# A state-space convolution beside a gated linear unit: the input's spectrum stored once, and its exchanged copy made by ScalarE

## The chip, the core and the metric

The kernel runs on one core of a Trainium2 chip. Its time is the device time of one execution in microseconds (us). The engines have these names in the profile: PE is TensorE (matmul), PEld its weight loads, DVE VectorE, ACT ScalarE, POOL GpSimd; SP issues all the transfers. The on-chip memory SBUF and the accumulators PSUM have 128 partitions.

## What is computed

With L = 2048 positions, D = 448 channels, N = 256 states and F = 1792 hidden units, all fp32:

```python
def _A_ref(u, log_A_real, A_imag, C_real, C_imag, log_dt, D_skip):   # L = 2048
    dt = jnp.exp(log_dt)
    A = -jnp.exp(log_A_real) + 1j * A_imag
    C = (C_real + 1j * C_imag) * dt[:, None]
    P = jnp.exp((A * dt[:, None])[:, :, None] * pos[None, None, :])
    K = 2.0 * jnp.einsum("dn,dnl->dl", C, P).real
    y = jnp.fft.irfft(jnp.fft.rfft(u_t, 2 * L) * jnp.fft.rfft(K, 2 * L), 2 * L)[:, :, :L]
    return y.transpose(0, 2, 1) + u * D_skip
def _B_ref(x, w_gate, w_up, w_down):
    h = _sigmoid(x @ w_gate) * (x @ w_up)
    return h @ w_down
g = _sigmoid((x * gate_w).sum(-1, keepdims=True))
return g * _A_ref(x, ...) + (1 - g) * _B_ref(x, ...)
```

Path A makes a long filter K for each channel and convolves u with it by Fourier transforms; path B is a gated linear unit (GLU) on the same input; a gate mixes the two.

## The kernel before

**Path A.** The channels are worked in two halves of 224. A transform of 4096 points is split into a stage of 64-point transforms (`stage1`, L812), an exchange of 32x32 blocks between partitions (`transpose`), and a stage of 32-point transforms (`spectrum_four`, L845). A `Chain` object carries one half through these stages in one tile `fx` of 128 x 32 x 224. A row of 64 partitions of a spectrum has 32 real rows and then 32 imaginary rows; the matrix `m_sb` holds the 32-point transform forwards, backwards, and a third form of it.

First the chains of u run, one for each half, in the pool `fu` (`fx_fu`). Their spectra go to DRAM, to `us0` and `us1`. Meanwhile `kgen` makes K in 28 chunks (tiles `tb`, `es`, `cs`, `nn`, `ke`) and stores it to `kd0` and `kd1`. Then the chains of K run: chain 0 in `fx_fu` with tiles `uax`, chain 1 in `fx_fk` with tiles `ua`. In `product` each takes eight blocks b: it loads the block of u's spectrum into a tile of [128, 2, 2, 448] (two buffers for each chain), makes the spectrum of K in PSUM by matmuls (L845), multiplies on DVE (L879), transforms back by matmuls (L889, `product_four`), and ACT evacuates into `fx` (L762). `back` does the last stage (L924) after another `transpose`, which chain 0 does through DRAM (`shf`) and chain 1 on DVE (L826).

A complex product needs each of K's rows times u's real part and times u's imaginary part. The kernel before stores the real rows of u's spectrum twice, one copy under the other, as c = 0, and the imaginary rows twice as c = 1. So `ua[:, 0]` is (real, real) and `ua[:, 1]` is (imaginary, imaginary), each loaded by a transfer of 448 KB, and the inverse transform of c = 1 uses the third matrix, `turned`.

**Path B.** `glu_up` (L1423 to L1428, tiles `gu`) and `glu_down` (L1443 to L1447, tiles `dn`) do the GLU in fp32 from rounded high and low parts: ACT rounds a part (`wh`, `vh`, `hh`, L1388 and L1414), DVE takes the remainder (`wl`, `vl`, `hl`), ACT does tanh (`sg`, L1407), and DVE sums up in `ob` (L1462). TensorE has GLU matmuls between the pieces of path A over the whole run, to the end.

**The order of the work.** The table `PLACE` gives each operation of each engine its place in that engine's queue, by engine, tile and priority; `Plan.order` merges these queues with a model of the costs, and `emit` writes the instructions out. An engine runs its queue strictly in this order. The numbers were found by a search outside of this file. All transfers are issued by SP, in its own order. The helper that records a transfer is line L712, and that of an evacuation L762.

Of the kernel before, what the change touches and what calls it, by code (L numbers as in the profile page):

```python
# [13 lines left out]
AF = mybir.ActivationFunctionType  # L14
# [4 lines left out]
L, D, N, F = 2048, 448, 256, 1792  # L19
# [9 lines left out]
    ('Act', 'aci', 10): (14, 40,),  # L29
    ('Act', 'aci', 19): (65, 94,),  # L30
    ('Act', 'acr', 10): (15, 39, 49,),
    ('Act', 'acr', 19): (63, 91, 101,),
# [26 lines left out]
    ('Act', 'dots', 1): (28,),  # L59
    ('Act', 'dots', 2): (45,),  # L60
    ('Act', 'dots', 16): (67, 83,),
# [18 lines left out]
    ('Act', 'idn', 10): (12,),  # L80
    ('Act', 'junk', 10): (29, 60,),
    ('Act', 'junk', 19): (77, 81, 132,),
# [12 lines left out]
    ('Act', 'pos_sb', 10): (36, 52,),  # L95
# [22 lines left out]
    ('DVE', 'aci', 10): (45,),  # L118
    ('DVE', 'aci', 19): (122,),
    ('DVE', 'acr', 10): (89,),  # L120
    ('DVE', 'acr', 19): (152,),
# [1467 lines left out]
```

## Time and profile before

| | |
|---|---|
| runs, median (lowest to highest of 3) | 688.12 us (686.7 to 689.95) |
| profiled execution | 684.96 us |
| its span, first to last instruction | 683.0 us |
| mean granted TensorE clock | 0.999 |
| moved by transfers | 122.79 MB, mean 180 GB/s |

The profile is of one execution. Its page gives the busy time of each engine, the chain of work that ended last, and groups of instructions; further views give waits, a timeline, and busy time by stage. In the timeline a row has a start, a duration (of all its instructions together, xcount), the engine, the line and the tiles, and in brackets the idle time ahead of it with what ended that. In a row of groups the numbers behind the bar are busy us and mean ns of one instruction. Rows of transfers have the size and the median time from issue to landing. Durations of one engine overlap: how fast a queue moves is seen from the distance of starts.

The stages by time: parameters and gate until about 115 us, `kgen` until 505 us with the chains of u in it, the products of both chains from 530 to 626 us, the transforms back from 647 us.

### The profile page before, as it was taken

To read this page: it belongs to the slowest core of one execution; us is meant where nothing else is said; L and a number is where in the kernel's file an instruction comes from. 1 tells how busy PE (TensorE), PEld (TensorE's weight loads), DVE (VectorE), ACT (ScalarE), POOL (GpSimd) and SP (SyncE) were. 2 spreads that over 40 slices of the span, in tenths; PEclk is the share of its full clock that TensorE was granted. 3 is DMA by queue.
4 is the path that set the end of the run, shared out by engine and by line. 5 is a ranking of instruction groups with operands and counts; after the bars stand their busy time and mean duration, and the time that the engine had idled before them with its cause. 6 is when DMAs were issued, how large, how long until landed. Compare 5 with 4: busy or idle time off the path is not lost.

```text
span 683.0 us, 16235 instructions
## 1 busy us (share of the span) xinstructions
PE 669.7 (98%) x6568; PEld 480.6 (70%) x6568; DVE 603.7 (88%) x699; ACT 509.7 (75%) x928; POOL 269.2 (39%) x280
## 2 busy tenths in 40 slices
PE   8899999999999999999989999999999999999997
PEld 7677667877886687776646666778878766546864
DVE  7998999999899999999998999999974379667976
ACT  6588799898999999999999999999842442333110
POOL 0506486555466656675856567643000000000000
PEclk9999999999999999999999999999999999999999
DMA  8869432683793999737977884343968981888855
GB/s 265 222 146 245 111 101 57 174 217 139 208 173 85 204 203 225 237 111 178 176 211 179 200 212 113 124 155 111 204 133 217 280 292 66 300 276 217 153 141 129
DMA packets 96898, 122.79 MB, mean 180 GB/s; under 512 B 31032, under 2 KB 80504, under 8 KB 95800
## 3 DMA queue, kind: packets, MB, share of 16 engines
q1 hardware_dynamic: 96824, 121.76, 69.7%
q8 instruction: 52, 0.85, 0.5%
q14 instruction: 22, 0.18, 0.1%
HBM read 78.16 MB, written 43.58 MB: 178 GB/s over the span
## 4 chain that ended last, share of the span: by engine, by line
PE 82%; DVE 10%; ACT 3%; DMA 2%; issue 2%; SPq 1%; DVEq 0%
PE gu_gps L1423 10%; PE gu_gps L1424 9%; PE gu_gps L1425 9%; PE kp_egp L1290 7%; PE dn_gps L1443 6%; PE dn_gps L1445 5%; PE tp_egp L1232 4%; PE tp_egp L1241 4%; PE dn_gps L1446 4%; PE dn_gps L1447 4%; PE fps_fups L812 3%; PE gu_gps L1427 3%; PE fps_fups L845 3%; PE gu_gps L1428 3%; PE fps_fups L889 2%; PE fps_fkps L889 2%
## 5 line engine op out<-in xcount | busy, mean ns | idle before, releaser
L1423 PE MATMUL gu_gps<-xs_glu,wh_glu 128*128 128x512 f32 x336 | 144.6, 430 | 1.6 <-DVE hl_glu L1409 0.8
L1278 DVE TENSOR_TENSOR cs_eg<-cs_eg,es_eg 128x2048 f32<-128x2048 f32 x56 | 131.5, 2349 | 1.4
L1424 PE MATMUL gu_gps<-xs_glu,wh_glu 128*128 128x512 f32 x336 | 132.0, 393 | 0.1
L1425 PE MATMUL gu_gps<-xs_glu,wl_glu 128*128 128x512 f32 x336 | 131.7, 392 | 0.0
L1222 POOL TENSOR_TENSOR tb_eg<-tb_eg 128x96 f32<-128x96 f32 (+2 forms) x84 | 118.8, 1416 | 6.1
L1261 DVE TENSOR_TENSOR es_eg<-tb_eg 128x1024 f32<-128x1024 f32 x112 | 110.4, 1013 | 2.1 <-POOL tb_eg L1222 0.5
L1423 PEld LDWEIGHTS gu_gps<-xs_glu,wh_glu 128*128 128x128 f32 x336 | 63.2, 188 | 30.8 <-issue 15.8
L1275 DVE TENSOR_TENSOR cs_eg<-cs_eg,es_eg 128x1024 f32<-128x1024 f32 x56 | 70.8, 1264 | 8.2 <-ACT cs_eg L1254 5.8
L1238 ACT ACTIVATE nn_eg<-cs_eg 128x512 fp32r<-128x512 f32 x112 | 74.9, 669 | 3.8 <-PE tp_egp L1241 2.6
L1407 ACT ACTIVATE sg_glu<-gu_gps 128x512 f32<-128x512 f32 x56 | 34.5, 615 | 55.2 <-PE gu_gps L1428 54.9
L1424 PEld LDWEIGHTS gu_gps<-xs_glu,wh_glu 128*128 128x128 f32 x336 | 63.3, 188 | 16.0 <-issue 5.0
L1425 PEld LDWEIGHTS gu_gps<-xs_glu,wl_glu 128*128 128x128 f32 x336 | 63.1, 188 | 14.4
L1243 ACT ACTIVATE cs_eg<-tp_egp 128x512 f32<-128x512 f32 x112 | 70.0, 636 | 3.1 <-PE tp_egp L1241 2.7
L1236 ACT ACTIVATE cs_eg<-tp_egp 128x512 f32<-128x512 f32 x112 | 69.9, 633 | 2.7 <-PE tp_egp L1232 1.0
L1244 ACT ACTIVATE cs_eg<-tp_egp 128x512 f32<-128x512 f32 x112 | 69.0, 627 | 1.1 <-PE tp_egp L1241 1.1
L1254 ACT ACTIVATE cs_eg<-cs_eg,half_pi 128x1024 f32<-128x1024 f32 x56 | 66.7, 1191 | 0.2
L1225 POOL TENSOR_TENSOR tb_eg<-tb_eg,bs_eg 128x32 f32<-128x32 f32 x84 | 62.6, 745 | 6.4
L1462 DVE SCALAR_TENSOR_TENSOR ob_glu<-dn_gps,og,ob_glu 128x448 f32<-128x448 f32 x70 | 47.4, 677 | 16.0 <-PE dn_gps L1447 15.1
L1290 PEld LDWEIGHTS kp_egp<-cs_eg 128*32 128x32 f32 x3584 | 51.3, 110 | 10.7 <-issue 7.6
L1212 POOL MEMSET tb_eg<- 128x96 f32 x28 | 8.0, 287 | 127.9 <-DVE es_eg L1261 124.8
L1290 PE MATMUL kp_egp<-cs_eg 128*32 128x64 f32 x3584 | 55.8, 220 | 0.0
L1241 PE MATMUL tp_egp<-nn_eg,idn 128*128 128x512 f32 x112 | 51.4, 459 | 1.2 <-ACT nn_eg L1238 1.2
(168 smaller groups left out, 1326.0 us busy)
## 6 DMA issues: line engine op xcount, KB each, us to landing
shf<-fx_fu SPq DMA_DIRECT2D x16, 896.0 KB, 5.4
fx_fu<-shf SPq DMA_DIRECT2D x16, 896.0 KB, 10.4
us<-fx_fu SPq DMA_DIRECT2D x16, 896.0 KB, 9.7
xr_glu<-in_w_dram SPq DMA_DIRECT2D x46, 256.0 KB, 6.1
uax_fk<-us SPq DMA_DIRECT2D x16, 448.0 KB, 4.3
ua_fk<-us SPq DMA_DIRECT2D x16, 448.0 KB, 6.0
xr_glu<-in_w_dram SPq DMA_DIRECT2D x17, 224.0 KB, 4.1
gt_pre<-in_u_dram SPq DMA_DIRECT2D x8, 448.0 KB, 6.9
```

Of the source, the lines that this page charges most:

```text
L1222: pool(96 * m, lambda n=n, m=m: G.tensor_mul(g3(n + 1, m), g3(1, m), g3(n, 1).to_broadcast([128, 32, 3, m])))
L1236: op("Act", c_act(512, True), lambda: S.activation(cs[:, 1, ds, 32:96], block(tp), AF.Copy, bias=MAGIC), [tp], [(cs, ("s", i))], prio)
L1238: op("Act", c_act(512), lambda: S.activation(block(nn), cs[:, 1, ds, 32:96], AF.Copy, scale=-1.0, bias=MAGIC), [(cs, ("s", i))], [nn], prio)
L1241: op("PE", c_mm(532), lambda: T.matmul(tp.real, idn.real, nn.real, start=False, stop=True, skip_group_check=True), [nn, idn], [tp], prio)
L1243: op("Act", c_act(512, True), lambda: S.activation(cs[:, 0, ds, 32:96], block(tp), AF.Abs), [tp], [(cs, ("c", i))], prio)
L1261: V.tensor_mul(o.rearrange("p d (i k) -> p d i k", k=ny), x.unsqueeze(3).to_broadcast([128, 16, nx, ny]), y.unsqueeze(2).to_broadcast([128 ...
L1275: op("DVE", c_dve(1024), lambda: V.tensor_mul(cs[:, :, :, 0:32], cs[:, ::-1, :, 63:31:-1], es[:, :, 0:32].unsqueeze(1).to_broadcast([128, ...
L1278: op("DVE", c_dve(2048), lambda: V.tensor_mul(cs[:, :, :, 32:96], cs[:, :, :, 32:96], es[:, :, 32:96].unsqueeze(1).to_broadcast([128, 2, 1 ...
L1290: T.matmul(kp[32 * j:32 * j + 32, q], cs[:, z, 4 * j + q, 64:96], cs[:, z, 4 * j + q, 0:64], start=cs is parts[0] and z == 0 and q == 0, s ...
L1423: T.matmul(p.real, wh[:, k, cs], x[:, k], start=(k == 0), stop=False)
L1424: T.matmul(p.real, wh[:, k, cs], x[:, 4 + k], start=False, stop=False)
L1425: T.matmul(p.real, wl[:, k, cs], x[:, k], start=False, stop=False)
```

## The change

The spectrum of u is stored as it is, with real rows over imaginary rows, once: four stores for each half in place of eight. `product` loads it once for each block, as `ua[:, 0]` = (real, imaginary). The second copy `ua[:, 1]` = (imaginary, real) is made on chip by `turn_parts`: for each of two halves z of the tile's columns, ACT copies four groups of 32 partitions to the neighbouring group. The tables follow: the product of c = 0 is now (real x real, imaginary x imaginary), and the signs are moved into the matrices. Lines behind the new function are 6 higher than before.

```diff
     inv[re, re], inv[im, re], inv[re, im], inv[im, im] = cw, -sw, sw, cw
-    turned[re], turned[im] = inv[im], -inv[re]
+    turned[re], turned[im] = inv[im], inv[im]
+    inv[im] = -inv[re]
...
-    us = [dt_([128, 2, 8, 2 * D], f"us{h}") for h in halves]
+    us = [dt_([128, 8, 2 * D], f"us{h}") for h in halves]
...
-            for q in range(2):
-                for g in range(2):
-                    for c in range(2):
-                        dma(lambda q=q, g=g, c=c: us[64 * g:64 * g + 64, c, 4 * q:4 * q + 4].rearrange(
-                                "(z k) b f -> k z (b f)", z=2),
-                            lambda q=q, g=g, c=c: x[64 * g + 32 * c:64 * g + 32 * c + 32, 16 * q:16 * q + 16].rearrange(
-                                "k l d -> k (l d)").unsqueeze(1).to_broadcast([32, 2, 8 * D]),
-                            64 * 16 * HD * 4, self.keys(8 * q, 8 * q + 8), [(us, (q, g, c))], prio, 215.0, 1400.0)
+            for q in range(4):
+                dma(lambda q=q: us[:, 2 * q:2 * q + 2].rearrange("p b f -> p (b f)"),
+                    lambda q=q: x[:, 8 * q:8 * q + 8].rearrange("p l d -> p (l d)"), 128 * 8 * HD * 4,
+                    self.keys(4 * q, 4 * q + 4), [(us, q)], prio)
...
                 ua = self.tile("ua", (128, 2, 2, D))
+                dma(lambda ua=ua: ua[:, 0].rearrange("p z f -> p (z f)"), lambda b=b: us[:, b], 128 * 2 * D * 4,
+                    [(us, b // 2)], [(ua, (0, 0)), (ua, (0, 1))], self.prio)
                 for c in range(2):
-                    dma(lambda ua=ua, c=c: ua[:, c].rearrange("p z f -> p (z f)"), lambda b=b, c=c: us[:, c, b],
-                        128 * 2 * D * 4, [(us, (b // 4, g, c)) for g in range(2)], [(ua, (c, 0)), (ua, (c, 1))], self.prio)
+                    self.turn_parts(ua, c)
                 self.product_four(ua, b)
...
+        def turn_parts(self, ua, z):
+            def f():
+                for a in range(0, 128, 32):
+                    to = a ^ 32
+                    S.activation(ua[to:to + 32, 1, z], ua[a:a + 32, 0, z], AF.Copy)
+            op("Act", 4 * c_act(D), f, [(ua, (0, z))], [(ua, (1, z))], self.prio)
```

The table `PLACE` has new numbers throughout, of which one line shows the kind:

```diff
-    ('SP', 'us0', 30): (135, 136, 132, 131, 140, 141, 139, 137,),
+    ('SP', 'us0', 30): (130, 135, 136, 138,),
```

ScalarE's queue in the middle of the products. Before, it holds the evacuations of the inverse transforms of both chains (L762), with a GLU instruction between (L1407 tanh, L1388 rounding):

```order
L762 ACTIVATE fx_fk_6562<-fps_fkps_7070 128x448
L762 ACTIVATE fx_fk_6562<-fps_fkps_7069 128x448
L1407 ACTIVATE sg_glu_7132<-gu_gps_7005 128x512
L762 ACTIVATE fx_fk_6562<-fps_fkps_7122 128x448
L762 ACTIVATE fx_fu_5091<-fps_fups_7134 128x448
L762 ACTIVATE fx_fk_6562<-fps_fkps_7121 128x448
L762 ACTIVATE fx_fu_5091<-fps_fups_7135 128x448
```

Now the copies of both chains (L879 of the new file) stand between the evacuations (L763 of the new file); this is the place of chain 1's blocks 5, 6 and 7 (`ua_fk_7272`, `7333`, `7392`):

```order
L879 ACTIVATE uax_fk_7285<-uax_fk_7285 32x448 x4
L763 ACTIVATE fx_fu_4932<-fps_fups_7349 128x448
L763 ACTIVATE fx_fu_4932<-fps_fups_7350 128x448
L763 ACTIVATE fx_fk_6536<-fps_fkps_7375 128x448
L879 ACTIVATE uax_fk_7285<-uax_fk_7285 32x448 x4
L879 ACTIVATE ua_fk_7333<-ua_fk_7333 32x448 x8
L879 ACTIVATE ua_fk_7392<-ua_fk_7392 32x448 x4
L763 ACTIVATE fx_fu_4932<-fps_fups_7436 128x448
L763 ACTIVATE fx_fk_6536<-fps_fkps_7376 128x448
```

The second evacuation of one block (`fps_fkps_7376`) now stands sixteen copies and an evacuation behind the first (`fps_fkps_7375`).

SP's queue in the same stretch. Before, two transfers for each block, among the stores of chain 0's `transpose` (`shf`):

```order
L712 DMA uax_fk_7080<-us_58 128x896
L712 DMA ua_fk_7090<-us_59 128x896
L712 DMA shf<-fx_fu_5091 128x1792
L712 DMA ua_fk_7090<-us_59 128x896
L712 DMA uax_fk_7080<-us_58 128x896
L712 DMA ua_fk_7145<-us_59 128x896
```

Now one for each, with loads of GLU weights (`xr`) between them:

```order
L713 DMA uax_fk_7019<-us_58 128x896
L713 DMA ua_fk_7066<-us_59 128x896
L713 DMA xr_glu_7069<-in_w_dram 128x512
L713 DMA uax_fk_7100<-us_58 128x896
L713 DMA xr_glu_7118<-in_w_dram 128x448
L713 DMA ua_fk_7126<-us_59 128x896
```

Each block's second transfer is gone; its place in the chain of a block is taken by the copies on ScalarE. In all SP's queue goes from 328 rows to 304, ScalarE's gets 128 instructions more, and TensorE's has the same 2,303 matmul rows in a new order.

More of the change, by code (lines that the diff above doesn't have):

```diff
@@ L28 @@
 PLACE = {
[L29 to L32, printed above, removed]
[26 rows of a table removed]
-    ('Act', 'dots', 1): (28,),
-    ('Act', 'dots', 2): (45,),
-    ('Act', 'dots', 16): (67, 83,),
[18 rows of a table removed]
-    ('Act', 'idn', 10): (12,),
-    ('Act', 'junk', 10): (29, 60,),
-    ('Act', 'junk', 19): (77, 81, 132,),
[12 rows of a table removed]
-    ('Act', 'pos_sb', 10): (36, 52,),
[13 rows of a table removed]
+    ('Act', 'aci', 10): (15, 41,),
+    ('Act', 'aci', 19): (67, 101,),
+    ('Act', 'acr', 10): (16, 38, 52,),
@@ L109 @@
+    ('Act', 'acr', 19): (64, 97, 110,),
[26 rows of a table added]
+    ('Act', 'dots', 1): (28,),
+    ('Act', 'dots', 2): (46,),
+    ('Act', 'dots', 16): (66, 80,),
[18 rows of a table added]
+    ('Act', 'idn', 10): (14,),
+    ('Act', 'junk', 10): (32, 60,),
+    ('Act', 'junk', 19): (76, 81, 136,),
[12 rows of a table added]
+    ('Act', 'pos_sb', 10): (35, 40,),
[11 rows of a table added]
+    ('Act', 'uax', 40): (829, 828, 842, 832, 852, 865, 871, 869, 883, 880, 898, 890, 906, 900, 916, 912,),
[3 rows of a table added]
     ('Act', 'wh', 0): (1, 4,),
     ('Act', 'wh', 1): (6, 7,),
[4 rows of a table removed]
[4 rows of a table added]
     ('Act', 'xs', 0): (0, 2, 3, 5,),
[2 rows of a table removed]
@@ L118 @@
-    ('DVE', 'aci', 10): (45,),
-    ('DVE', 'aci', 19): (122,),
[2 rows of a table added]
+    ('DVE', 'aci', 10): (49,),
+    ('DVE', 'aci', 19): (128,),
     ('DVE', 'acr', 10): (89,),
-    ('DVE', 'acr', 19): (152,),
[2 rows of a table removed]
+    ('DVE', 'acr', 19): (153,),
[2 rows of a table added]
     ('DVE', 'bsx0', 10): (90, 109,),
[1 row of a table removed]
[1 row of a table added]
     ('DVE', 'ci', 10): (71,),
[1 row of a table removed]
[1 row of a table added]
     ('DVE', 'cr', 10): (69, 73,),
[8 rows of a table removed]
[8 rows of a table added]
     ('DVE', 'dtp', 10): (30,),
     ('DVE', 'dtv', 10): (27,),
[6 rows of a table removed]
[6 rows of a table added]
     ('DVE', 'f', 10): (14, 15,),
[1 row of a table removed]
[1 row of a table added]
     ('DVE', 'gs', 1): (53,),
[5 rows of a table removed]
-    ('DVE', 'half_pi', 0): (9,),
[24 rows of a table removed]
-    ('DVE', 'ones', 10): (1,),
@@ L179 @@
-    ('DVE', 'p', 10): (18, 20, 21, 22, 23, 25, 26,),
-    ('DVE', 'phs', 20): (2,),
[6 rows of a table removed]
-    ('DVE', 'skip', 20): (0,),
[6 rows of a table removed]
-    ('DVE', 'uax', 40): (539, 534, 546, 547, 556, 557, 570, 571, 578, 575, 585, 586, 590, 591, 595, 596, 624, 623,
[34 rows of a table removed]
[5 rows of a table added]
+    ('DVE', 'half_pi', 0): (1,),
[24 rows of a table added]
+    ('DVE', 'ones', 10): (0,),
+    ('DVE', 'p', 10): (16, 17, 18, 19, 21, 22, 24,),
+    ('DVE', 'phs', 20): (3,),
[6 rows of a table added]
+    ('DVE', 'skip', 20): (2,),
[6 rows of a table added]
+    ('DVE', 'uax', 40): (534, 531, 547, 548, 554, 561, 570, 569, 578, 576, 583, 582, 589, 588, 594, 595, 622, 623,
[34 rows of a table added]
```

521 rows, old and new, of the table PLACE are left out of this document.

## The prediction

> **What bounds the kernel now.** I read the page first: the busy time of the engines and the chain that ended last.
>
> ```profile
> span 683.0 us, 16235 instructions
> PE 669.7 (98%) x6568; PEld 480.6 (70%) x6568; DVE 603.7 (88%) x699; ACT 509.7 (75%) x928; POOL 269.2 (39%) x280
> PE 82%; DVE 10%; ACT 3%; DMA 2%; issue 2%; SPq 1%; DVEq 0%
> ```
>
> TensorE is busy for 98% of the span and carries 82% of the chain; transfers carry 2% of it. A busy matmul row overlaps its neighbours, so the timeline has to say whether the busy time is full of work, and the table by stage where it is not.
>
> ```profile
> 571.23 0.39 PE L1423 MATMUL gu_gps<-xs_glu,wh_glu 128*128 128x512 f32 x1
> 571.46 0.39 PE L1424 MATMUL gu_gps<-xs_glu,wh_glu 128*128 128x512 f32 x1
> 571.69 0.39 PE L1425 MATMUL gu_gps<-xs_glu,wl_glu 128*128 128x512 f32 x1
> ...
> 0.00:60.00 60.00, 56.02 (x228) 42.16 (x229) 53.55 (x114) 42.02 (x74) 17.25 (x16) 1.00 0.83 221
> 60.00:115.00 55.00, 53.55 (x201) 36.35 (x199) 52.96 (x80) 48.13 (x82) 36.35 (x35) 1.00 0.42 110
> 115.00:330.00 215.00, 214.94 (x2772) 160.37 (x2772) 208.80 (x202) 205.34 (x377) 128.31 (x134) 1.00 0.72 177
> 330.00:346.00 16.00, 14.75 (x292) 9.90 (x292) 15.75 (x13) 15.57 (x29) 12.73 (x11) 1.00 1.01 181
> 573.00:626.00 53.00, 53.00 (x411) 26.76 (x410) 36.63 (x41) 18.50 (x36) 0.00 (x0) 1.00 0.75 250
> 645.00:683.00 38.00, 32.26 (x210) 22.53 (x208) 28.05 (x56) 2.46 (x4) 0.00 (x0) 0.99 0.50 122
> ```
>
> Each matmul shows 0.39 us, but the next one starts 0.23 us later, without a hole: the queue is full. The columns of the stages are the stretch, its length, then busy time of PE, PEld, DVE, ACT and POOL, the granted clock, the DMA share and GB/s. TensorE is idle for 683.0 - 669.7 = 13.3 us in all, at both ends and around 330 to 346, where DVE and ACT are both full. From 573 to 626, the stretch where both spectra are multiplied, it is never idle and ACT works 18.5 of 53 us. What TensorE does wait for:
>
> ```profile
> PE dn_gps L1443 <- DVE ob_glu L1462: 1.3, 2, 0.8
> PE tp_egp L1241 <- ACT nn_eg L1238: 1.2, 1, 1.2
> ...
> PE dn_gps L1443 <- DMA vh_glu<-in_w_dram: 0.5, 1, 0.5
> ```
>
> These are three of ten rows, 8.3 us in all (total, times, longest); one of them is a transfer, of GLU weights, 0.5 us. No row names the spectrum `us`.
>
> [...]
>
> **What the change removes.** The rows of its transfers:
>
> ```profile
> us<-fx_fu SPq DMA_DIRECT2D x16, 896.0 KB, 9.7
> uax_fk<-us SPq DMA_DIRECT2D x16, 448.0 KB, 4.3
> ua_fk<-us SPq DMA_DIRECT2D x16, 448.0 KB, 6.0
> q1 hardware_dynamic: 96824, 121.76, 69.7%
> DVE uax_fk L879 <- DMA uax_fk<-us: 2.8, 2, 2.6
> 280.00:300.00 20.00, 3.77 (x6) 1.00 0.54 178
> 330.00:346.00 16.00, 3.58 (x6) 1.00 1.01 181
> ```
>
> Eight of the 16 stores go (7.3 MB) and 16 of the 32 loads (7.3 MB), 14.7 of 121.8 MB; SP issues 24 transfers fewer. On the path that is worth 0 us: the one wait for `us` is DVE's 2.8 us ahead of a product (L879), in a stretch where TensorE was never idle because GLU matmuls covered it. That cover is the reason for the zero; without it 2.8 us would return. Nor do engines run faster with less traffic: the last two rows are ACT's L1243 alone, six instructions each, 0.63 us at a DMA share of 0.54 and 0.60 at 1.01. I bound the indirect gain by 0 and by the 1.25 us that TensorE idles between 330 and 346, where all DMA queues are full; I take 0, since ACT and DVE are themselves full there (15.6 and 15.8 of 16).
>
> TensorE's own work is unchanged: the same 2,303 matmul rows, and 177 changes between array shapes in either order, so no term comes from there. The new matrices in `m_sb` have the old size. The new sequences before 505 us move work between full engines (ACT 205 and DVE 209 of 215 us); their sum is unchanged, and I set them at 0, with both signs left to the rivals.
>
> **What it adds: 128 ScalarE copies of 32x448.** No row has this shape. The nearest:
>
> ```profile
> 547.87 0.58 ACT L1388 ACTIVATE vh_glu<-xr_glu 128x448 fp32r<-128x448 f32 x1 [1.63 <-PE dn_gps L1446]
> 500.64 1.03 ACT L1388 ACTIVATE vh_glu<-xr_glu 128x448 fp32r<-128x448 f32 x2
> 516.02 1.14 ACT L1388 ACTIVATE wh_glu<-xr_glu 128x512 fp32r<-128x512 f32 x2
> L762 ACT ACTIVATE fx_fk<-fps_fkps 128x448 f32<-128x448 f32 x16 | 8.1, 542 | 7.4 <-PE fps_fkps L889 7.4
> 584.26 0.98 ACT L762 ACTIVATE fx_fu<-fps_fups 128x448 f32<-128x448 f32 x2 [3.20 <-PE fps_fups L889]
> 573.59 1.74 PE L889 MATMUL fps_fups<-uax_fk,m_sb 64*64 64x448 f32 x16
> 576.01 0.50 PE L1423 MATMUL gu_gps<-xs_glu,wh_glu 128*128 128x512 f32 x1
> 576.34 0.39 PE L1424 MATMUL gu_gps<-xs_glu,wh_glu 128*128 128x512 f32 x1
> 624.45 1.74 PE L889 MATMUL fps_fkps<-ua_fk,m_sb 64*64 64x448 f32 x16
> L879 DVE TENSOR_TENSOR ua_fk<-ua_fk,fps_fkps 128x896 f32<-128x896 f32 x16 | 16.7, 1082 | 7.1 <-PE fps_fkps L845 7.1
> 500.00:530.00 30.00, 30.00 (x259) 24.66 (x259) 15.85 (x24) 8.88 (x17) 0.00 (x0) 1.00 0.76 184
> 530.00:575.00 45.00, 45.00 (x262) 31.76 (x264) 31.17 (x32) 17.87 (x35) 0.00 (x0) 1.00 0.72 217
> 630.00:645.00 15.00, 15.00 (x70) 12.92 (x70) 14.88 (x13) 3.52 (x6) 0.00 (x0) 1.00 1.15 197
> ```
>
> A copy of 448 columns from SBUF to SBUF takes 0.58 us alone, a second one behind it 0.45 more. In a queue I take 0.47 (two in 1.03, less the shared 0.1 at the end); the ends are 0.44, which is the second of two PSUM evacuations (0.98 - 0.54, L762), and 0.58, no overlap at all. A quarter of the partitions is taken to cost what all cost, since the columns are what the time scales with. So a turn of one half (`turn_parts`, four copies) is 1.88 us, one block of 8 copies 3.75 us, and all 16 blocks 60 us. Before 573 us they hide: ACT works 26.8 of the 75 us from 500 to 575, and the first blocks of both chains are turned there.
>
> From chain 0's third block of inverse matmuls (573.59) to chain 1's last (624.45) they don't. Before, this is 50.9 us of TensorE. In the new order the same piece has 7 more 128x512 matmuls (7 x 0.23 = 1.6) and 4 more shape changes (about 0.1 each: the first start after one is 0.33 instead of 0.23 us long, 576.01 to 576.34): 52.9 us. In the same piece ACT's queue has 20 half turns (80 x 0.47 = 37.6 us), 25 evacuations (x 0.44 = 11.0) and 5 GLU instructions (x 0.52, by the second of two `wh` rows, = 2.6): 51.2 us. It can't begin at once: its first row evacuates the block that TensorE starts with (1.6 us), and the first turn waits for a load into the buffer that this block frees, 4.3 us to land, of which ACT fills 2.5 with its other rows; 1.8 us idle. Behind its last turn stands a product on DVE, 1.08. So the last inverse matmuls can start at 1.6 + 1.8 + 51.2 + 1.1 = 55.7 us, and TensorE would be there at 52.9: **2.8 us late**. With 0.44 per copy it comes to 53.3, 0.4 late; with 0.58 to 64.5, 11.6 late.
>
> Queued behind the turns on ACT are the evacuations of both chains' PSUM banks. Chain 1 has three banks; near the end the evacuation of block 5's second half stands behind four half turns, and block 6's inverse matmuls need that bank if banks go round in turn. Chain 1's products, the last three blocks above all, are what TensorE then waits for. After this piece the order is as before: 95 GLU matmul rows, while DVE transposes, then the last transform; DVE fills 630 to 645, so no cover there takes up a delay, and it reaches the end.
>
> Sum: the profiled execution took 684.96 us (683.0 of span and 1.96 around it); + 2.8 - 0 = 687.8. The runs shown have a median of 688.12, 3.2 above that execution; on the median it is 690.9 us, +0.4%. A measurement here can tell about 0.5%, 3.4 us, from no change.
>
> **Rivals.** *ACT becomes the bound outright (slower).* If the copies don't overlap, or loads land late behind SP's other issues, the piece runs at ACT's pace: 11.6 us at the most, about 8 (696 us) with half of the overlap. For it: a turn adds 3.75 us to a ring of two buffers per chain. Against: four copies in a row wait for nothing between them. It decides from 0.49 us per copy on (80 x 0.02 + 2.8 = 4.4).
>
> *The lighter queue and the new order pay (faster).* Of TensorE's 13.3 idle us, the start and the tail can't go:
>
> ```profile
> 1.18 2.08 PE L1039 MATMUL fps_fups<-ones_pro 112*128 112x128 f32 x8 [1.18 <-DVE ones_pro L1034]
> 677.86 0.37 PE L1447 MATMUL gu_gps<-vl_glu,hh_glu 128*128 128x448 f32 x1
> ```
>
> 1.2 ahead of the first matmul and 4.8 after the last leave 7.3. If an order with less traffic to dodge takes back 60% of it and keeps the turns fed, that is -4.4: 683.7 us. For it: DMA is full at 330 to 346, where TensorE idles 1.25, and the prologue loses 5.4 us. Against: no wait there names `us`, and the prologue holds none of the change. [...]
>
> *The turns hide (no change).* If the first loads land early and copies cost 0.44, the 0.4 us is covered: 688.5 us. For it: ACT has 34.5 idle us in the piece; against: 51.2 of new queue in 52.9.
>
> **How the numbers follow.** My forecast, 1 to 5 us more, 0.45, of which 0.12 lies above 3.4 us; outright ACT bound 0.24; hidden 0.09; faster 0.22. That makes faster 0.22, same 0.33 + 0.09 = 0.42, slower 0.36. The forecast's own range is 689 to 693; to leave out no more than 2 in 10 the range reaches to the faster rival's 683.5 and to 698, short of the bound of 11.6.
>
> **What would show it.** L879 copies of about 0.57 us, 0.47 apart when queued, 60 us in all; ACT above 90% from the third block to the last, and rows where PE, or DVE's products ahead of it, wait for ACT's `ua` turns, 2 to 4 us, mostly in chain 1's last blocks; q1 near 107 MB; the time before 505 us within 2 us of now. I am wrong if copies are far from 0.47 us, if TensorE is never idle there, or if the first 505 us move by more than 3 us.

## The result, and the profile after

The changed kernel takes 704.56 us (median of 4 runs, 704.14 to 705.08) and the kernel before, timed beside it, 689.04 us (686.7 to 690.29): a ratio of 1.0237, 95% interval 1.0201 to 1.0273. It is slower, by 15.5 us; the forecast was 690.9 with a range up to 698. The page after:

```profile
span 703.1 us, 16348 instructions
...
PE 682.6 (97%) x6568; PEld 481.3 (68%) x6568; DVE 601.4 (86%) x699; ACT 582.7 (83%) x1056; POOL 275.3 (39%) x280
...
q1 hardware_dynamic: 94392, 107.08, 57.7%
...
PE 67%; ACT 18%; DVE 7%; DMA 4%; issue 3%; SPq 0%; ACTq 0%; DVEq 0%
```

The transfers are 14.7 MB lighter, as the change says. ACT's share of the chain went from 3% to 18%, TensorE's from 82% to 67%. Where that is, the table by stage shows (columns as before: stretch, length, then PE, PEld, DVE, ACT, POOL, clock, DMA share, GB/s):

```profile
115.00:330.00 215.00, 214.82 (x2651) 159.17 (x2650) 209.35 (x198) 204.36 (x376) 133.67 (x133) 1.00 0.58 156
...
500.00:530.00 30.00, 29.96 (x259) 24.60 (x258) 15.29 (x22) 12.58 (x23) 0.00 (x0) 1.00 0.74 187
530.00:575.00 45.00, 42.35 (x232) 29.32 (x231) 26.06 (x28) 40.23 (x74) 0.00 (x0) 1.00 0.53 154
573.00:626.00 53.00, 50.07 (x331) 25.45 (x333) 33.19 (x35) 44.92 (x82) 0.00 (x0) 1.00 0.38 123
575.00:630.00 55.00, 52.07 (x351) 25.74 (x353) 32.21 (x35) 48.39 (x88) 0.00 (x0) 1.00 0.40 129
630.00:645.00 15.00, 12.34 (x75) 5.50 (x71) 7.03 (x7) 14.62 (x28) 0.00 (x0) 1.00 0.30 101
```

Up to 530 us TensorE is as busy as before. From 530 on it is not: 42.35 of 45 us and 12.34 of 15, where it had no idle time before, and its busy time is thinner than it looks, with 331 matmul records from 573 to 626 where there were 411. ACT is busy 40 of 45, 48 of 55 and 14.6 of 15 us. The stretch from 575 to 630, on which the experiments below are compared, had this row before:

```profile
575.00:630.00 55.00, 55.00 (x413) 29.18 (x406) 38.09 (x43) 18.37 (x36) 0.00 (x0) 1.00 0.80 257
```

The copies, in the groups of instructions (behind the bar busy us and mean ns of one):

```profile
L879 ACT ACTIVATE uax_fk<-uax_fk 32x448 f32<-32x448 f32 x64 | 36.8, 575 | 1.3 <-DMA uax_fk<-us 0.3
L879 ACT ACTIVATE ua_fk<-ua_fk 32x448 f32<-32x448 f32 x64 | 36.8, 575 | 0.9
```

One takes 575 ns, as forecast. But 64 of 575 ns are 36.8 us: the busy time, which counts an overlap once, is the plain sum. Copies that follow each other don't overlap. The timeline of ACT shows it at one place, and those of TensorE and DVE what waits behind:

```profile
598.57 4.67 ACT L879 ACTIVATE ua_fk<-ua_fk 32x448 f32<-32x448 f32 x8
603.26 0.54 ACT L763 ACTIVATE fx_fk<-fps_fkps 128x448 f32<-128x448 f32 x1
```

```profile
603.86 0.97 PE L846 MATMUL fps_fkps<-fx_fk,m_sb 64*64 64x448 f32 x4 [0.90 <-ACT fx_fk L763]
```

```profile
604.93 1.09 DVE L885 TENSOR_TENSOR ua_fk<-ua_fk,fps_fkps 128x896 f32<-128x896 f32 x1 [6.34 <-ACT fx_fk L763]
```

Eight copies fill 4.67 us, so their starts are (4.67 - 0.575) / 7 = 0.585 us apart; over the whole kernel 108 pairs of queued copies lie 0.583 to 0.603 apart, median 0.587. At 0.47 the eight would have ended 0.8 us sooner. The evacuation of a PSUM bank stands behind them, TensorE waits 0.90 us for that bank, and DVE has stood idle for 6.34 us when it gets to chain 1's next product. The waits of TensorE (total, times, longest) name the evacuations first:

```profile
PE fps_fkps L846 <- ACT fx_fk L763: 3.1, 5, 0.9
...
PE fps_fkps L895 <- DVE ua_fk L885: 1.4, 1, 1.4
```

The piece of the forecast, from chain 0's third block of inverse matmuls to chain 1's last, lies between these rows of TensorE:

```profile
578.57 0.97 PE L895 MATMUL fps_fups<-uax_fk,m_sb 64*64 64x448 f32 x6
...
644.86 1.36 PE L895 MATMUL fps_fkps<-ua_fk,m_sb 64*64 64x448 f32 x12
```

It takes 66.3 us, where 50.9 were taken before and 55.7 forecast, and it starts 5.0 us later than before (573.59). Behind it lie 58.2 us to the end, as before (58.6). ACT's first row in it starts at 580.33, after 4.3 us of waiting for the piece's first matmuls; from there to the end of the piece ACT is busy for 62.2 of 64.5 us. So its queue is all but full.

Each of the two rows is the start of a block of 16 matmuls, and counts only those in a short window.

### The profile page after: what moved, and what is told of

It is laid out like the page before. It is cut to its first block, busy times and chain, and to the rows that moved or that the text cites. A ratio compares the mean times of both kernels' runs of the same rounds, so it can differ in the third digit from the quotient of the medians.

```text
span 703.1 us, 16348 instructions
## 1 busy us (share of the span) xinstructions
PE 682.6 (97%) x6568; PEld 481.3 (68%) x6568; DVE 601.4 (86%) x699; ACT 582.7 (83%) x1056; POOL 275.3 (39%) x280
## 3 DMA queue, kind: packets, MB, share of 16 engines
q1 hardware_dynamic: 94392, 107.08, 57.7%
## 4 chain that ended last, share of the span: by engine, by line
PE 67%; ACT 18%; DVE 7%; DMA 4%; issue 3%; SPq 0%; ACTq 0%; DVEq 0%
PE gu_gps L1429 8%; PE gu_gps L1430 8%; PE gu_gps L1431 8%; PE dn_gps L1449 7%; PE kp_egp L1296 6%; ACT ua_fk L879 5%; PE tp_egp L1238 4%; ACT uax_fk L879 4%; PE tp_egp L1247 3%; PE dn_gps L1451 3%; PE fps_fups L813 3%; PE dn_gps L1452 3%; PE dn_gps L1453 3%; PE gu_gps L1433 3%; PE gu_gps L1434 3%
## 5 line engine op out<-in xcount | busy, mean ns | idle before, releaser
L1228 POOL TENSOR_TENSOR tb_eg<-tb_eg 128x96 f32<-128x96 f32 (+2 forms) x84 | 115.1, 1371 | 6.6
L1267 DVE TENSOR_TENSOR es_eg<-tb_eg 128x1024 f32<-128x1024 f32 x112 | 108.0, 986 | 2.2
L1231 POOL TENSOR_TENSOR tb_eg<-tb_eg,bs_eg 128x32 f32<-128x32 f32 x84 | 76.5, 913 | 6.2
L1431 PEld LDWEIGHTS gu_gps<-xs_glu,wl_glu 128*128 128x128 f32 x336 | 63.4, 189 | 14.6
```

The source lines that it names most:

```text
L1228: pool(96 * m, lambda n=n, m=m: G.tensor_mul(g3(n + 1, m), g3(1, m), g3(n, 1).to_broadcast([128, 32, 3, m])))
L1231: pool(32, lambda e=e: G.tensor_mul(t(e + 1), t(e), b(3)))
L1267: V.tensor_mul(o.rearrange("p d (i k) -> p d i k", k=ny), x.unsqueeze(3).to_broadcast([128, 16, nx, ny]), y.unsqueeze(2).to_broadcast([128 ...
L1431: T.matmul(p.real, wl[:, k, cs], x[:, k], start=False, stop=False)
```

## The experiments

All edits but one are made in the changed kernel. The theories, as the expectations name them: **A**, ScalarE's queue is the loss, because a copy that starts at other partitions than the instruction ahead of it doesn't overlap with that; **B**, the new order or late loads; **C**, the shift between a copy's input and output; **D**, any copy of 32 partitions; **E**, the length of a row of copies between evacuations; **F**, a delay of each product in proportion to its copies. Each ratio is to the kernel before as timed beside that run.

| run | us, median | ratio to the kernel before, 95% |
|---|---|---|
| the changed kernel | 704.56 | 1.0237 (1.0201 to 1.0273) |
| four whole copies into one place | 701.32 | 1.0223 (1.0178 to 1.0267) |
| one whole copy | 688.21 | 1.0012 (0.9993 to 1.003) |
| four straight copies of 32 | 705.44 | 1.0272 (1.0249 to 1.0295) |
| paired | 711.6 | 1.0379 (1.0346 to 1.0413) |
| four whole copies, places apart | 689.13 | 1.0005 (0.998 to 1.0031) |
| three copies | 689.31 | 1.0006 (0.9979 to 1.0033) |
| half of the copies on GpSimd | 688.79 | 1.0008 (0.998 to 1.0036) |
| the kernel before, one store and one load | 687.96 | 1.0003 (0.9971 to 1.0035) |
| five whole copies, places apart | 701.99 | 1.022 (1.0179 to 1.0262) |
| all copies on GpSimd | 690.93 | 1.0059 (1.0028 to 1.009) |
| wide copies | 704.34 | 1.0252 (1.0207 to 1.0297) |

**Four whole copies into one place.**

```diff
-                for a in range(0, 128, 32):
-                    to = a ^ 32
-                    S.activation(ua[to:to + 32, 1, z], ua[a:a + 32, 0, z], AF.Copy)
+                for a in range(4):
+                    S.activation(ua[:, 1, z], ua[:, 0, z], AF.Copy)
```

> Each half turn is four copies of all 128 partitions straight across (128x448, no exchange of rows), in place of four copies of 32 partitions; so the exchange is left out, and the number and place of ScalarE's instructions is that of the changed kernel. Theory A: the copies cost 0.587 us because each starts at another partition than the one before it, which keeps them from overlapping; then these start 0.47 us apart as queued 128x448 copies did in the kernel before, the turns take 7.5 us less in the piece from chain 0's third inverse block to chain 1's last (20 half turns x 4 x 0.117 = 9.4 us of ScalarE's queue), and the time is 691 to 695 us. Theory B: the 13 us come from the new order and late loads, not from the copies' price; then it stays at 702 to 706 us.

701.3 us: neither theory's number, and the run doesn't separate them. All four copies write the same place, so the program makes each wait on ScalarE's own semaphore for the write of the one before. Within a half turn they start 0.61 us apart (median), and 0.48 from one half turn to the next, where there is no such wait. The run with places apart, below, differs from this one in where three of the four copies write.

**One whole copy** for each half turn: the loop above becomes the one line `S.activation(ua[:, 1, z], ua[:, 0, z], AF.Copy)`.

> Each half turn is one copy of 128x448 straight across; the exchange is left out, 96 of 128 copies are gone, the order and the transfers are those of the changed kernel. Theory A (ScalarE's copies are the whole loss): 686 to 690 us, as the kernel before, since ScalarE's queue in the piece falls from about 63 to 26 us. Theory B (order, single load): it stays above 698 us. If the single store and load or the new order pay by themselves, it lies below 686 us.

```profile
575.00:630.00 55.00, 55.00 (x404) 27.89 (x401) 36.03 (x42) 28.36 (x57) 0.00 (x0) 1.00 0.54 162
```

688.2 us: with the changed kernel's order, single store and single load, and 96 copies fewer, the loss is gone, and TensorE is never idle in the stretch. B falls. What is left of the change gains nothing either.

**Four straight copies of 32 partitions**: `to = a ^ 32` becomes `to = a`.

> Four copies of 32 partitions for each half turn as in the changed kernel, but each straight across to its own 32 partitions; the exchange is left out. Theory A (another start partition than the instruction before): still 0.58 to 0.60 us apart and 702 to 706 us. Theory C (the shift between in and out is what costs): 0.47 us apart and 691 to 695 us. Theory D (any copy of 32 partitions takes 0.587 us): as theory A.

```profile
598.95 3.50 ACT L878 ACTIVATE ua_fk<-ua_fk 32x448 f32<-32x448 f32 x6
```

(3.50 - 0.575) / 5 = 0.585 us apart, and 705.4 us. C falls: there is no shift here, only a change of partitions from one copy to the next.

**Paired**: the same eight copies, ordered so that two in a row have the same partitions.

```diff
-                for a in range(0, 128, 32):
+                for a in (64 * z, 64 * z + 32):
                     to = a ^ 32
-                    S.activation(ua[to:to + 32, 1, z], ua[a:a + 32, 0, z], AF.Copy)
+                    for y in range(2):
+                        S.activation(ua[to:to + 32, 1, y], ua[a:a + 32, 0, y], AF.Copy)
...
+for _k in (('Act', 'ua', 41), ('Act', 'uax', 40)):
+    PLACE[_k] = tuple(min(PLACE[_k][i - i % 2], PLACE[_k][i - i % 2 + 1]) + i % 2 / 2 for i in range(16))
```

> The same eight copies of 32x448 for a block with the exchange, in another order: the two halves of the columns of one group of 32 partitions one behind the other, and all eight in one place of ScalarE's queue (that of the first half turn). Theory A: within a pair the second copy starts 0.47 us behind the first, between pairs 0.587 us, mean 0.53; ScalarE's queue in the piece is 40 x 0.117 = 4.7 us shorter, so 699 to 702 us. Theories C and D: 0.587 us throughout and 703 to 708 us.

```profile
605.43 2.09 ACT L882 ACTIVATE uax_fk<-uax_fk 32x448 f32<-32x448 f32 x4
607.54 4.19 ACT L882 ACTIVATE ua_fk<-ua_fk 32x448 f32<-32x448 f32 x8
```

The spacing is A's: 0.48 to 0.49 within each of the 64 pairs, 0.57 to 0.58 between them, and eight copies take 4.19 us instead of 4.67. D falls, since these too are copies of 32 partitions. The time is a miss: 711.6 us where I had 699 to 702. In the changed kernel a block's second half turn stands further back in the queue; put ahead, it holds evacuations up. One place in the trace shows it: where the changed kernel has eight copies between two evacuations of chain 1 (548.50 to 553.17), this run has sixteen (549.78 to 558.18), and TensorE stands idle 3.39 us for the evacuation behind them. Its granted clock is 0.66 from 560 to 565, just behind that, and 1.00 in the changed kernel. So the piece starts 6.4 us later than in the changed kernel, though it is 2.1 us shorter: a shorter queue in a worse order lost more. What the order and what the clock costs, no run separates.

**Four whole copies, places apart**: as the first run, but three of the four write to constants that are no longer read, which are made 128 partitions tall.

```diff
+                S.activation(ua[:, 1, z], ua[:, 0, z], AF.Copy)
+                for to in (pos[:, 0:D], pos[:, 512:512 + D], phs.v("p a n -> p (a n)").bitcast(F32R)[:, 0:D]):
+                    S.activation(to, ua[:, 0, z], AF.Copy)
```

> As the four copies of all 128 partitions for each half turn, but each writes to a place of its own (one to the second copy of the spectrum, three to constant tiles that are no longer read), so that none waits for the write of the one before; the exchange is left out. This is my forecast's own sum with its own price. Theory A: copies start 0.47 to 0.48 us apart, ScalarE's queue in the piece is 51 to 52 us long against 52.9 of TensorE, the piece takes about 55.7 us and the time is 688 to 693 us. Theory E (the price per copy is not the reason, but the length of ScalarE's row of work between two evacuations): the copies are at 0.47 but the time stays above 697 us.

```profile
596.91 0.60 ACT L877 ACTIVATE uax_fk<-uax_fk 128x448 f32<-128x448 f32 x1
597.38 1.07 ACT L879 ACTIVATE pos_sb<-uax_fk 128x448 fp32r<-128x448 f32 x2
598.32 0.60 ACT L879 ACTIVATE phs<-uax_fk 128x448 fp32r<-128x448 f32 x1
598.78 0.60 ACT L877 ACTIVATE ua_fk<-ua_fk 128x448 f32<-128x448 f32 x1
```

```profile
573.69 1.34 PE L895 MATMUL fps_fups<-uax_fk,m_sb 64*64 64x448 f32 x10
...
628.84 1.36 PE L895 MATMUL fps_fkps<-ua_fk,m_sb 64*64 64x448 f32 x12
```

The same 128 instructions in the same places, 0.467 us apart, and 689.1 us. This run has the price that I forecast, and it gives the forecast's piece: it starts at 573.69 and takes 55.15 us (55.7 worked out). Against the changed kernel's profile (span 703.1 to 687.3) the 15.8 us are 4.9 before the piece, 11.1 in it and -0.2 behind it. E falls: there are as many copies between two evacuations as in the changed kernel. For comparison, the piece takes 53.8 us in the run with one copy, and as much in the one with half of the copies on GpSimd: that is what TensorE itself needs in this order.

**Three copies**: one of 64 partitions straight, two of 32 exchanged, each starting elsewhere than the one before.

```diff
+                S.activation(ua[0:64, 1, z], ua[0:64, 0, z], AF.Copy)
+                for a in (64, 96):
+                    to = a ^ 32
+                    S.activation(ua[to:to + 32, 1, z], ua[a:a + 32, 0, z], AF.Copy)
```

> Three copies for each half turn, each at other partitions than the one before (one of 64 partitions straight across, two of 32 with the exchange); the exchange of the other 64 partitions is left out, 96 copies in place of 128. Theory A: 0.587 us apart, ScalarE's queue in the piece is 20 x 3 x 0.587 + 11 to 14 for the other rows = 46 to 49 us, which fits into TensorE's 52.9, so most of the loss is gone: 688 to 693 us. Theory F (each copy delays its own product, so the loss grows in proportion to the copies): 705 - 32 / 96 x 16 = about 699 us.

```profile
575.00:630.00 55.00, 54.84 (x398) 28.00 (x397) 35.49 (x41) 52.30 (x96) 0.00 (x0) 1.00 0.53 163
```

These are 0.588 us apart (median), and still the time is 689.3 us: a quarter of the copies less, and the whole loss is gone. The piece takes 54.6 us. F falls; a queue that just fits costs nothing that can be measured, and ACT works 52.3 of 55 us, which shows how close that is.

**Patterns**, for the spacing alone (one run, 694.8 us). What is copied, by half and chain, stands in the expectation.

> Four patterns of four copies in the place of the four copies of a half turn, for the spacing of starts alone; the exchange is left out or replaced. Chain 0, first half: from the same 32 partitions to four others in turn. Chain 0, second half: one of 128 partitions, then from three groups in turn to the same 32 partitions. Chain 1, first half: 128, 32, 128, 32 partitions, all starting at partition 0. Chain 1, second half: 64 partitions at 0, 64 at 64, 64 at 0, 64 at 0. Theory A in its narrow form (another start partition of input or output keeps two instructions apart): 0.587 in the first two, 0.48 in the third, and 0.587, 0.587, 0.48 in the fourth. Theory A in its wide form (any change of the set of partitions): 0.587 in the third as well. Theory C (a shift between in and out costs): the fourth is 0.48 throughout.

```profile
588.61 0.57 ACT L891 ACTIVATE ua_fk<-ua_fk 128x448 f32<-128x448 f32 x1
589.07 0.56 ACT L892 ACTIVATE pos_sb<-ua_fk 32x448 fp32r<-32x448 f32 x1
589.54 0.56 ACT L893 ACTIVATE pos_sb<-ua_fk 128x448 fp32r<-128x448 f32 x1
590.01 0.56 ACT L894 ACTIVATE phs<-ua_fk 32x448 fp32r<-32x448 f32 x1
590.48 0.56 ACT L887 ACTIVATE uax_fk<-uax_fk 128x448 f32<-128x448 f32 x1
591.06 1.18 ACT L889 ACTIVATE pos_sb<-uax_fk 32x448 fp32r<-32x448 f32 x2
592.26 0.58 ACT L889 ACTIVATE phs<-uax_fk 32x448 fp32r<-32x448 f32 x1
592.86 0.58 ACT L891 ACTIVATE ua_fk<-ua_fk 128x448 f32<-128x448 f32 x1
```

128, 32, 128, 32, 128 partitions, all starting at partition 0, are 0.46 to 0.47 us apart: 32 or 128 partitions make no difference here. Copies to partition 0 from partitions 32, 64 and 96 (L889) are 0.60 apart, and so is the next one that starts at 0 again. The other two patterns agree: the same input to four places in turn 0.588, and 64-partition copies starting at 0, 64, 0, 0 are 0.58, 0.598 and 0.483 apart. So a change of the start of either the input or the output is enough: A in its narrow form.

**Half of the copies on GpSimd**, with the exchange complete.

```diff
+                    if z:
+                        G.tensor_copy(ua[to:to + 32, 1, z], ua[a:a + 32, 0, z])
+                    else:
                         S.activation(ua[to:to + 32, 1, z], ua[a:a + 32, 0, z], AF.Copy)
```

> The second half turn of each block is copied by GpSimd, which is idle from 505 us on, the first by ScalarE as in the changed kernel; the exchange is complete. ScalarE's queue in the piece falls by 10 x 4 x 0.587 = 23.5 us to about 40. Theory A: the loss is gone if GpSimd keeps up; its copies are bounded by 0.80 us (the 128x96 operation) and 1.74 us (the 128x448 product), 40 copies in the piece are 32 to 70 us against 52.9, so 687 to 692 us with 1.2 us or less for a copy and up to 708 us with 1.74. Theory B (order and loads): 700 us or more whatever GpSimd's copies take.

```profile
L883 POOL COPY ua_fk<-ua_fk 32x448 f32<-32x448 f32 x32 | 18.5, 577 | 25.8 <-DMA ua_fk<-us 16.4 <-PE fps_fkps L849 3.2 <-PE gu_gps L1443 3.0
```

```profile
575.00:630.00 55.00, 54.99 (x407) 27.49 (x404) 37.11 (x43) 42.02 (x78) 22.89 (x40) 1.00 0.51 158
```

688.8 us. A GpSimd copy takes 0.577 us, below the 0.80 that I had as its bound; ACT works 42 and GpSimd 23 of the 55 us, and TensorE is never idle.

**The kernel before, with one store and one load** and nothing in their place: the removed half of the change by itself.

```diff
-                    for c in range(2):
+                    for c in range(1):
                         dma(lambda q=q, g=g, c=c: us[64 * g:64 * g + 64, c, 4 * q:4 * q + 4].rearrange(
...
-                for c in range(2):
+                for c in (1,):
...
-                    ua[:, :, z], ua[:, :, z], p[z][:, :D].unsqueeze(1).to_broadcast([128, 2, D])),
+                    ua[:, :, z], ua[:, 1:2, z].to_broadcast([128, 2, D]), p[z][:, :D].unsqueeze(1).to_broadcast([128, 2, D])),
```

> The kernel before, in its own order, with the spectrum stored once and loaded once for each block and nothing put in the place of the rest: 8 stores and 16 loads gone, no copy added; both products read the one part that is loaded, so the second one's data are left out. This is the removed half of the change alone. My forecast's 0: within 0.3% of the kernel before (686.5 to 690.5 us), bounds 0 to 1.25 us faster. The rival of the lighter queue: 2 to 4.4 us faster.

```profile
q1 hardware_dynamic: 93880, 107.08, 62.2%
```

12% of the bytes gone, and a ratio of 1.0003 (0.9971 to 1.0035), that is, between 2.0 us faster and 2.4 us slower: worth nothing that can be measured. The bound of 1.25 us lies within that interval and stays open; the rival's 2 to 4.4 us lie at its edge and beyond.

**Five whole copies, places apart**: a fifth copy, 0.467 us apart, so that a half turn holds ScalarE as long as four unlike copies do.

> As the four copies of all 128 partitions with places of their own, but five for each half turn; the exchange is left out. They start 0.467 us apart, so a half turn fills ScalarE for 5 x 0.467 = 2.34 us, as four copies 0.587 us apart do (2.35). Theory A in full (only the time that a half turn holds ScalarE's queue counts, not the partitions themselves): as the changed kernel, 702 to 707 us. If the 32-partition copies harm in another way as well (their write ports, DVE's products, latency): 688 to 697 us.

```profile
575.00:630.00 55.00, 53.01 (x359) 26.05 (x357) 32.52 (x35) 49.18 (x106) 0.00 (x0) 1.00 0.42 131
```

702.0 us, a ratio of 1.022 beside the changed kernel's 1.0237, with no copy of 32 partitions and no change of start in it. The piece takes 64.3 us and starts at 578.8. At the same places in the queue, what counts is the time for which a half turn holds it. That the places count too, the paired run shows.

**All copies on GpSimd**: the branch of the half before, for both halves.

> All 128 copies of the exchange on GpSimd, 0.60 us apart there as in the run with half of them; ScalarE's queue is that of the kernel before. GpSimd has 80 x 0.60 = 48 us in the piece, without evacuations between them, against 52.9 us of TensorE. Theory A (the loss is a full queue that also carries the evacuations of PSUM): 688 to 693 us. If the latency of a turn is the loss, whoever makes it: 698 to 705 us.

```profile
607.51 4.76 POOL L884 COPY ua_fk<-ua_fk 32x448 f32<-32x448 f32 x8
```

```profile
575.00:630.00 55.00, 53.76 (x396) 26.61 (x392) 34.87 (x40) 17.71 (x37) 45.09 (x80) 1.00 0.51 157
```

690.9 us, 0.6% above the kernel before. A block's turn takes 4.76 us there, longer than on ScalarE, and yet most of the loss is gone: no evacuation stands behind it there. The 0.6% may come from GpSimd's own queue, which works 45 of the 55 us: DVE waits 12.3 us in all for its copies there, and the piece takes 55.3 us, against 53.8 with half of them. No run separates that.

**Wide copies**: both halves of the columns in one copy of 32x896, in the places of the paired run.

```diff
-                for a in range(0, 128, 32):
+                for a in (64 * z, 64 * z + 32):
                     to = a ^ 32
-                    S.activation(ua[to:to + 32, 1, z], ua[a:a + 32, 0, z], AF.Copy)
+                    S.activation(ua[to:to + 32, 1].rearrange("p z f -> p (z f)"), ua[a:a + 32, 0].rearrange("p z f -> p (z f)"), AF.Copy)
```

> Four copies of 32x896 for each block in place of eight of 32x448, both halves of the columns in one, all four in the place of the first half turn, as in the run with the paired copies (711.6 us). Each starts at other partitions than the one before: 0.587 + 448 x 0.8 ns = 0.95 us apart, 3.8 us for a block against 4.2 there. Theory A for ScalarE's queue alone would give 10 x (4.7 - 3.8) = 9 us less than the changed kernel, 695 to 697 us; if what made the paired run slower is the place (a whole block's turn ahead of evacuations, behind one load), it is 10 x 0.4 = 4 us less than that run, 705 to 709 us.

```profile
599.09 3.83 ACT L881 ACTIVATE uax_fk<-uax_fk 32x896 f32<-32x896 f32 x4
```

0.96 us apart, that is (0.96 - 0.587) / 448 = 0.83 ns for each added column where 0.8 was expected, 3.83 for a block, and 704.3 us: 7 us less than the paired run and no better than the changed kernel. It lies between my two numbers, just below the second. Beside the changed kernel's profile, the piece starts 2.8 us later and is 5.0 us shorter: the place takes back part of what the shorter queue gains. Here too the granted clock is 0.66 for a while before the piece (555 to 560).

No run beats the kernel before. The version with half of the copies on GpSimd equals it with 12% fewer bytes, and beats the changed kernel by some 16 us.

## Why the prediction was wrong

- **The price of a copy: the step that failed.** I took 0.47 us, from second rows of pairs that both start at partition 0, and argued for it that "four copies in a row wait for nothing between them". The columns do set a copy's own length (0.575 us in 32 partitions, as forecast, and 0.56 to 0.58 in 128 in the run with the patterns), but the overlap of 0.11 us is lost at every change of partitions: 0.587, the median of the 108 queued pairs. The 80 copies in the piece are 80 x 0.12 = 9.6 us longer by that, of the 11.1 us that lie between this piece and the one with copies at 0.467. "No overlap at all" was in the forecast as an end of 0.58, and 0.49 as the point from which ACT decides; I chose the wrong one of two ends between which the rows shown couldn't tell.
- **The worst case was too small too.** By 0.58 I had 11.6 us late. Measured, the piece is 66.3 - 52.9 = 13.4 us late (12.5, by the 53.8 us that TensorE needed). The evacuations next to copies lose their overlap as well: a copy behind an evacuation starts 0.55 us or more after it, and an evacuation behind a copy 0.60, where I had 0.44 for all 25.
- **"Before 573 us they hide"** fell with the same price: the piece starts 4.9 us later than at 0.467. These 4.9 us and the 11.1 in the piece make up the whole loss, and I had cut the range at 698, short of the bound's 699.7.
- **Right: the place; the sum in part by luck.** ACT's queue in the piece holds the 80 copies and 25 evacuations of the forecast. With the price as assumed, the piece takes 55.15 us where 55.7 was worked out, but terms in it were off and in part made up for each other: 8 GLU rows, not 5, and after its first row ACT was idle for 0.8 us, not 1.8. TensorE itself needed 53.8 us, not 52.9, so at 0.467 the piece was 1.4 us late, half of the 2.8. The whole run gives no more than that: its interval, 0.998 to 1.0031, holds 0 and ends at 2.1 us.
- **A slip in the working.** With half of the overlap a copy takes 0.525 us, which by the same sum is 7.2 us late, not "about 8".
- **Right: the removed half.** 14.7 MB less are worth nothing, within 2.4 us; q1 is at 107.08 MB; TensorE is idle for as long up to 505 us as before (7.2 us, before 7.6). The lighter queue and the new order pay nothing that shows.
- **Partly right: what waits.** I named the evacuations behind the copies and the last blocks of chain 1. TensorE's rows name the evacuations (3.1 us), and DVE's products wait 8.5 us for the copies; but the chain of waits goes through the copies from 539 us on, ahead of the piece and all through it, not only at its end.

## What to carry to other kernels

Price an added instruction by its place in the queue, not only by its length: look whether the rows from which you take the pace have the same start partitions as the new ones (0.467 us apart here with equal starts, 0.587 with unequal ones), and if no row does, let the range reach to the plain sum of durations, and count the rows next to the new ones in it. Here ScalarE's idle time had room up to a sharp edge: 96 copies 0.588 us apart cost nothing (689.3 us) and 128 cost 15.5 us (704.6), because the evacuations that TensorE needs stand in the same queue. Half of the copies cost nothing on GpSimd, which was idle there (688.8 us), and transfers that no wait of TensorE named went away without any gain (688.0 us, a ratio of 1.0003).

## What the runs showed of ScalarE

In this kernel's runs ScalarE overlaps an instruction with the one ahead of it by about 0.11 us only if the input starts at the same partition as the last input from that memory (SBUF or PSUM), and the output at the same as the last output. I took the starts from the programs (0, 32, 64 or 96) and sorted by this all pairs of ScalarE instructions behind 505 us that follow each other without a gap, in the two kernels and seven of the runs: of 698 pairs with a change none overlaps; of 709 without one 706 do. The memory of the input matters in the run with straight copies: a copy that starts at partition 0 behind an evacuation from PSUM, which starts there too, is 0.55 to 0.61 us behind it when the last copy within SBUF started at partition 96, and 0.42 when a GLU row within SBUF lay between. With equal starts copies of 448 columns overlap by 575 - 467 = 108 ns, with unequal ones not at all.

Two smaller ones: a wait on ScalarE's own write just ahead costs the overlap as well (0.61 us apart beside 0.467), and a copy of 32x448 is as fast on GpSimd as on ScalarE (0.577 us, 0.60 apart; on ScalarE 0.575 and 0.587).
